# The FFT stage of a gated S4 and dense-layer backward pass: four groups' powers in one written order, with room of its own for the second group's squares

## The chip, the cores and the metric

The kernel is written in Bass and Tile for one Trainium2 chip and runs on one of its cores. The metric is the time of one execution on the device in microseconds (us), as the median of several runs; less is better. The engines are called PE (TensorE, matrix products), DVE (VectorE), ACT (ScalarE), POOL (GpSimd) and SP (SyncE, which here only issues DMAs). ACT and POOL issue DMAs too. Each engine works through its own list of instructions in order, and waits on semaphores where an instruction needs something that another engine or a DMA must have done.

## The reference

The reference is a forward and a backward pass. A gate `g` mixes two branches of an input `x` of 2048 positions by 448 channels: a state-space convolution, computed by FFT, and a dense layer with a squared ReLU. Cut to what matters here:

```python
def _A_ref(u, A_re, A_im, B_re, B_im, C_re, C_im, log_dt, Dskip):
    dt = jnp.exp(log_dt)[:, None]
    logdA = dt * (A_re + 1j * A_im)
    dB = dt * (B_re + 1j * B_im)
    P = jnp.exp(logdA[:, :, None] * l[None, None, :])
    K = jnp.einsum("dn,dnl,dn->dl", C_re + 1j * C_im, P, dB).real
    ...
    Yf = rfft2(u, zero-padded to 2 * L) * rfft2(K, zero-padded to 2 * L)
    return irfft2(Yf)[:, :, 0, :L] + u * Dskip
def _B_ref(x, w1, b1, w2, b2):
    r = relu(x @ w1 + b1)
    return (r * r) @ w2 + b2
def _fwd_reference(x, ...):
    g = sigmoid((x * gate_w).sum(-1, keepdims=True))
    return g * _A_ref(x, ...) + (1 - g) * _B_ref(x, ...)
out, vjp = jax.vjp(_fwd_reference, all arguments but B_x)
return (out, *vjp(grad_out))
```

`P` holds, for each of 448 channels and 256 states, the powers of one complex number for 2048 positions. The kernel never writes `P` out: it squares the complex numbers eleven times (levels k = 0 to 11, the powers 1, 2, 4, ... 2048) and builds small tables from the levels.

## The kernel before, in words

**Where the change lies.** The program has a start (loads, the first FFT step of `U` and of the gated gradient `DA`, the transposed copies), the FFT stage that the change touches, a long periodic stage (the tables of 14 chunks of channels between the steps of the dense layer), and an end (weight gradients, inverse FFTs, outputs). Up to the line `tc.manual_schedule()` a scheduler orders the instructions; from there on each engine's order is the order in which the code is written. The last instructions of the start, the transposed copies, are merged with the first of the FFT stage.

**Powers.** `powers(gr)` (L572) is a generator for one group of four chunks of channels (the fourth group has two). It yields once after a first copy (L583) and once after each of the levels k = 0 to 11, 13 steps in all. A level copies the present power into the group's record (L588, ACT), squares real and imaginary part into a scratch buffer `sqr` (L597, ACT), multiplies them into the next imaginary part (L598, DVE) and subtracts the squares for the next real part (L599, DVE). Level k = 4 adds four products on DVE (L591 to L594). Behind the last level POOL stores the record to HBM (`rec_d`, L602). Groups one and three keep their record in the tile `F` (`F17`) and their squares in `P` (`P14`, `W0` in the code). Groups two and four keep record and powers in `R` (`R32`, `RA`), and their squares in `S` (`S25`, `SB`). Each of these tiles had another use just before: the staged output of the first FFT step of `DA` lies in `R[0:10752]` until it is stored to HBM (`gd<-R`), and two blocks of the transposed gradient lie in `S[8192:12288]` until they are spilled to HBM (`DBT_d<-S`, L478). Right behind the stage `F` and `R` become the room of the tables.

**Spectra, products, inverse.** `load_spectrum(q, w)` loads a quarter q of what the first FFT step stored for `U` (w = 0, into tile `X`) or `DA` (w = 1, into `Y`). `spectrum(q, w, between)` makes the quarter's spectrum on PE in four pieces (`fwd2_steps`, L269), each emptied from PSUM by casts on ACT and DVE (L218, L219, L228, L230) into the tile `K`, and calls `between` after each; then POOL stores it (`sp<-K`, L624). The products of the two spectra (L293, DVE) go to the tile `D`, the first inverse step (L308, PE) takes them from there, and SP stores its result (`hd<-st` or `hd<-S`, L312).

**The order.** `levels` is the row of all groups' steps, and `PW(n)` takes the next n of it. Before, `pair_of` runs groups one and two in turn, step by step, and then three and four; a generator's end counts as a step of its own. There are 6 steps ahead of the first spectrum, 4 in it, 8 ahead of the second, 4 in it, 4 behind it, 4 in each of the six spectra that follow, and the rest (`PW(100)`) behind the loop. So groups one and two are done (26 levels' steps) when the first products begin, and the last levels of three and four come behind the last inverse step.

**Behind the stage.** SP loads the first chunk's record (`rec<-rec_d`, L741) and the stage's results (`D<-hd`, `P<-hd`, L317); DVE seeds the tables with copies (L728, L729, L764); ACT spreads the record's levels into `F` (L749 to L760); DVE builds the tables (L696, L697, L710 to L719); meanwhile POOL fills `X`, `Y`, `R` and `K` with constants (L677 to L683), once these tiles are free.

Of the kernel before, what the change touches and what calls it, by code (L numbers as in the profile page):

```python
# [32 lines left out]
NLEV = 12  # L33
RS = 1792
# [299 lines left out]
def kernel(ctx, tc, A_u, A_A_re, A_A_im, A_B_re, A_B_im, A_C_re, A_C_im, A_log_dt, A_Dskip,  # L334
# [124 lines left out]
    SB = K.t("S25", [P, 12800])  # L459
# [21 lines left out]
    RA = K.t("R32", [P, 16384])  # L481
# [9 lines left out]
    W0 = K.t("P14", [P, 7168])  # L491
# [76 lines left out]
    def powers(gr):  # L568
        nch = min(4, NCH - 4 * gr)
        cs_ = slice(4 * gr, 4 * gr + nch)  # L570
        n = nch * W2
        rb, cb, qb = psets[gr % 2]  # L572
        R = rb.rearrange("p (c r) -> p c r", c=4)[:, 0:nch]
        sd, lx, ly = fields(R)
        cur = [cb[:, 1024 * i:1024 * i + 1024].bitcast(fp32) for i in range(2)]
        sqr = qb.bitcast(fp32)

        def halves(ap):
            return ap[:, 0:2 * n].rearrange("p (t c w) -> p t c w", t=2, w=W2)

        def paired(ap):
            return ap[:, 0:2 * n].rearrange("p (c t w) -> p c t w", t=2, w=W2)
        S.copy(sd[:, :, 1], Wt[:, cs_])  # L583
        yield
        x, y = Lam[:, :, cs_], halves(cur[0])
        for k in range(NLEV):
            dst = sd[:, :, 3] if k == 3 else sd[:, :, 4] if k == 11 else sd[:, :, 0] if k == 4 else lx[..., LEVX[k]] if k in LEVX else ly[..., LEVY[k]]
            S.copy(dst.rearrange("p c t w -> p t c w"), x)  # L588
            if k == 4:
                ua, va = paired(cur[k % 2]), paired(sqr)  # L590
                V.tensor_tensor(out=ua, in0=Wt[:, cs_], in1=x[:, 0].unsqueeze(2).to_broadcast([P, nch, 2, W2]), op=ALU.mult)  # L591
                V.tensor_tensor(out=va, in0=Wt[:, cs_], in1=x[:, 1].unsqueeze(2).to_broadcast([P, nch, 2, W2]), op=ALU.mult)
                V.tensor_tensor(out=sd[:, :, 2, 0], in0=ua[:, :, 0], in1=va[:, :, 1], op=ALU.subtract)
                V.tensor_tensor(out=sd[:, :, 2, 1], in0=ua[:, :, 1], in1=va[:, :, 0], op=ALU.add)  # L594
            if k < NLEV - 1:
                sq = halves(sqr)
                S.activation(sq, x, ACT.Square)  # L597
                V.scalar_tensor_tensor(out=y[:, 1], in0=x[:, 0], scalar=2.0, in1=x[:, 1], op0=ALU.mult, op1=ALU.mult)  # L598
                V.tensor_tensor(out=y[:, 0], in0=sq[:, 0], in1=sq[:, 1], op=ALU.subtract)  # L599
                x, y = y, halves(cur[1 - k % 2])  # L600
            yield
        G_.dma_start(bass.AP(tensor=rec_d, offset=4 * gr * P * RS, ap=[[RS, P], [P * RS, nch], [1, RS]]), R)  # L602
# [12 lines left out]
    def load_spectrum(q, w):  # L615
        s1s[q, w] = s1r[(2 * q + w) % 4]
        K.load_s1(gd[w], q, s1s[q, w], G_ if w == 0 and q < 2 else None)

    def spectrum(q, w, between):
        sp = spw[:, 2 * (q % 2) + w]  # L620
        for _ in K.fwd2_steps(s1s[q, w], q, sp):
            between()
        dst = bass.AP(tensor=sp_d[w], offset=q * 4 * 2 * D, ap=[[16 * 2 * D, P], [1, 8 * D]])
        G_.dma_start(dst, sp.rearrange("p a r d -> p (a r d)"))  # L624

    def pair_of(g0, g1):
        live = [powers(g0), powers(g1)]
        while live:
            for g in list(live):
                if next(g, None) is None and g.gi_frame is None:  # L630
                    live.remove(g)
                    yield
                else:
                    yield
    levels = (x for g in ((0, 1), (2, 3)) for x in pair_of(*g))

    def PW(n=1):
        for _ in range(n):
            next(levels, None)
# [439 lines left out]
    for e in range(6):  # L1079
# [4 lines left out]
        for l in range(2 if e < 2 else 1):  # L1084
            q = G_ if (e + l) % 2 == 0 else nc.scalar
# [385 lines left out]
    def between(n):  # L1471
        Fl(1)
        Pg(1)
# [209 lines left out]
```

## Time and profile before

| What | Value |
|---|---|
| median of 3 runs | 812.24 us (810.79 to 814.69) |
| the profiled execution's own time | 809.82 us |
| its span in the profile | 808.0 us |
| mean granted TensorE clock | 0.879 |
| busy PE, DVE, ACT, POOL | 605.8, 614.0, 538.1, 169.5 us |
| FFT stage, first square of the second group to the last store | 88.14 to 180.32 us |

All times in the profile count from the start of the span. In a row of the instructions in order of time stand the start, the duration, the engine, the line of the code, the operation, what it writes and reads by the program's tile names, shapes, and in brackets how long the engine stood idle just before and what released it. `x2` means that two such instructions are merged into one row. A row with an engine name and a `q` is the queue of that engine, where a DMA is issued.

### The profile page before, as it was taken

The numbers are of one execution on the slowest core, as the hardware profiler recorded it, in microseconds if no ns is written. First come the engines' busy times: TensorE is split into PE (matmuls) and PEld (weight loads), VectorE is DVE, ScalarE is ACT, GpSimd is POOL, SyncE is SP. The second block draws the span as 40 slices with busy tenths as digits, with TensorE's granted clock in tenths as the row PEclk, the third lists the DMA queues.
The fourth block names the chain that finished last, engine by engine and source line by source line (L and its number), as shares of the span: only waits on it lengthen the run. The fifth ranks groups of instructions, "written<-read, shape, count | busy, mean of one in ns | idle before, by whom it ended". The sixth has DMA issues, their size and how long they took to land. (4 is left out here: it accounts for less than half of the span.)

```text
span 808.0 us, 17098 instructions
## 1 busy us (share of the span) xinstructions
PE 605.8 (75%) x6845; PEld 301.0 (37%) x6845; DVE 614.0 (76%) x947; ACT 538.1 (67%) x879; POOL 169.5 (21%) x276
## 2 busy tenths in 40 slices
PE   3677225562377889888988879889779688898987
PEld 1223002220143334443654435444545344444443
DVE  3793576996943989899799989998639692888355
ACT  0695585662378596868899779886467478455464
POOL 1222010005402130323231201011115321123212
PEclk9985556775678899999989999999989899999999
DMA  9978529449759197859875997898569999999982
GB/s 192 242 205 285 207 109 370 152 176 320 210 95 215 61 220 141 176 125 227 165 188 100 306 193 146 193 269 195 170 203 330 399 266 325 300 291 346 252 266 67
DMA packets 166318, 175.73 MB, mean 217 GB/s; under 512 B 104069, under 2 KB 144991, under 8 KB 165647
## 3 DMA queue, kind: packets, MB, share of 16 engines
q1 hardware_dynamic: 144376, 101.56, 50.4%
q0 software_dynamic: 19664, 70.21, 26.9%
q10 hardware_dynamic: 2198, 2.87, 1.6%
q8 instruction: 53, 0.87, 0.5%
q14 instruction: 27, 0.21, 0.1%
HBM read 83.67 MB, written 67.53 MB: 187 GB/s over the span
## 5 line engine op out<-in xcount | busy, mean ns | idle before, releaser
L857 ACT CAST P<-psF 128x1024 bf16<-128x1024 f32 x56 | 57.2, 1021 | 26.9 <-PE psF L855 26.7
L696 DVE TENSOR_TENSOR F<-X,F 128x1024 bf16<-128x1024 bf16 (+2 forms) x42 | 64.5, 1536 | 13.2 <-ACT X L729 8.0
L923 PEld LDWEIGHTS <-U 128*128 128x128 bf16 x448 | 40.6, 100 | 49.2 <-issue 14.6
L928 POOL DMA_DIRECT2D br_d<-D x32 | 17.5, 548 | 178.4 <-ACT D L927 173.4
L923 PE MATMUL psN<-D,U 128*128 128x448 bf16 x224 | 52.8, 378 | 2.6 <-DVE U L955 1.4
L1240 PEld LDWEIGHTS <-S 128*128 128x128 bf16 x416 | 38.9, 98 | 38.3 <-issue 9.1
L1240 PE MATMUL psX<-D,S 128*128 128x449 bf16 x224 | 47.2, 353 | 1.7 <-ACT S L1246 1.5
L923 PE MATMUL psN<-S,U 128*128 128x448 bf16 x224 | 46.8, 353 | 1.7 <-issue 1.5
L1003 PE MATMUL psN<-S,K 128*128 128x512 bf16 x168 | 42.4, 386 | 6.4 <-ACT R L830 5.9
L867 DVE TENSOR_TENSOR M<-P,psF 128x2048 bf16<-128x2048 bf16 x28 | 34.0, 1215 | 14.2 <-PE psF L813 12.8
L855 PE MATMUL psF<-R,S 41*32 41x256 bf16 x896 | 24.6, 291 | 26.3 <-DVE P L868 16.2
L1231 ACT ACTIVATE S<-psN 128x1024 bf16<-128x1024 bf16 x32 | 33.0, 1030 | 15.1 <-PE psN L1227 15.1
L1240 PE MATMUL psX<-K,S 128*128 128x448 bf16 x192 | 41.7, 362 | 1.5 <-ACT S L1243 1.5
L945 PE MATMUL psN<-S,K 128*128 128x512 bf16 x168 | 42.7, 392 | 0.2 <-ACT U L952 0.2
L269 PEld LDWEIGHTS <-M 128*64 128x64 bf16 x192 | 13.5, 127 | 73.8 <-issue 66.1
L697 DVE TENSOR_TENSOR X<-F 128x512 bf16<-128x512 bf16 (+2 forms) x42 | 35.6, 847 | 1.4
L1008 ACT ACTIVATE U<-psN 128x512 bf16<-128x512 f32 x56 | 31.0, 612 | 7.8 <-PE psN L1006 5.3
L836 ACT COPY S<-K 128x128 bf16<-128x128 bf16 x56 | 35.0, 1009 | 0.0
L868 DVE TENSOR_TENSOR P<-P,psF 128x2048 bf16<-128x2048 bf16 x28 | 34.2, 1221 | 1.0
L813 PE MATMUL psF<-ident,X 128*128 128x128 bf16 x448 | 32.6, 231 | 2.9 <-ACT P L857 2.7
L927 ACT CAST D<-psN 128x448 bf16<-128x448 f32 x32 | 17.4, 545 | 22.9 <-PE psN L923 22.8
L813 PEld LDWEIGHTS <-X 128*128 128x128 bf16 x448 | 28.7, 104 | 9.6 <-issue 8.4
(353 smaller groups left out, 1611.1 us busy)
## 6 DMA issues: line engine op xcount, KB each, us to landing
hd<-st SPq DMA_DIRECT2D x18, 448.0 KB, 3.1
sp<-K POOLq DMA_DIRECT2D x8, 896.0 KB, 4.0
dhT_d<-U SPq DMA_DIRECT2D x28, 256.0 KB, 5.4
R<-sp SPq DMA_DIRECT2D x8, 896.0 KB, 11.5
S<-dhT_d POOLq DMA_DIRECT2D x14, 512.0 KB, 7.2
R<-hd SPq DMA_DIRECT2D x16, 448.0 KB, 8.8
S<-rT_d POOLq DMA_DIRECT2D x12, 512.0 KB, 7.3
rec<-rec_d POOLq DMA_DIRECT2D x11, 448.0 KB, 4.8
```

The source lines that it names most:

```text
L696: V.tensor_tensor(out=Vt[:, 0:2 * w * n], in0=run(lo, 0, [0, 2], [NA, w], [1, n]), in1=run(PX[:, 0:1], 512 * k, [2, w], [0, n], [1, 2]), o ...
L697: V.tensor_tensor(out=run(lo, n, [NA * X2, 2], [NA, X2], [1, n]), in0=run(vb, 0, [n * X2, 2], [n, X2], [1, n]), in1=run(vb, (w + X2) * n, ...
L813: T_.transpose(ps[:, t, 128 * b:128 * b + 128], Xs[c % 2][:, o_:o_ + 128], ident[:])
L836: S.copy(D2[:, :, 0, 4 * l:4 * l + 4].rearrange("p (g i) a -> p a g i", g=NG), DK[:, l::4].rearrange("p a (e g q i) -> p a e q g i", g=NG, ...
L857: S.copy(zbs[c, g // 2][:, :, g % 2].rearrange("p t h k n -> p t k h n"), psz[:].rearrange("p t (k h n) -> p t k h n", k=2, h=2))
L867: V.tensor_tensor(out=pr.rearrange("p t g h k n -> p t (g h k n)"), in0=zv, in1=xv, op=ALU.mult)
L868: V.tensor_tensor(out=zv, in0=zv, in1=rev_dim(xv, 1), op=ALU.mult)
L923: T_.matmul(ps[:, 0:D], lhsT=hblk[:, j, P * tt:P * tt + P], rhs=ws[:, j, :], start=(w == 1 and j == 0), stop=(j == FT - 1))
L945: T_.matmul(pss[k][:], lhsT=w1w[:, dt, j * P:j * P + P], rhs=UT[:, dt, 512 * lb:512 * lb + 512], start=(dt == 0), stop=False, skip_group_c ...
L1003: T_.matmul(pss[k][:], lhsT=w2Tw[:, jp, dt, k], rhs=dblk[:, dt], start=(dt == 0), stop=False, skip_group_check=True)
L1231: S.activation(hn(i)[:, 8 * th:8 * th + 8, :], ps[:], ACT.Square if i < FT else ACT.Copy)
L1240: T_.matmul(ps[:, 0:w], lhsT=hn(i)[:, t, :], rhs=(DB2[:, t, :] if i < FT else U[:, t, 0:w]), start=(t == 0), stop=(t == LT - 1))
```

## The change

Three things change, all in the FFT stage. The squares of groups two and four move from `SB[:, 10240:11264]` to `RA[:, 10752:11776]`, behind the staged output. `pair_of` goes, and a list of turns takes its place: group one alone for seven steps (its first copy and k = 0 to 5), then groups one and two in turn for six steps each, then group two alone for its last seven (k = 5 to 11), then groups three and four in turn. The end of a generator, with its store, now belongs to its last step, so there are 52 steps and not 56. And they are handed out differently: 6 steps ahead of the first spectrum, 4 in it and 6 behind it make the sixteen ahead of the second spectrum, which has none; then two after each piece in the loop's first two rounds, one in the third, and none in the last.

```diff
-    psets = [(Fp[:, 0:4 * RS], RA[:, 14336:16384], W0[:, 3584:4608]), (RA[:, 0:4 * RS], RA[:, 8704:10752], SB[:, 10240:11264])]
+    psets = [(Fp[:, 0:4 * RS], RA[:, 14336:16384], W0[:, 3584:4608]), (RA[:, 0:4 * RS], RA[:, 8704:10752], RA[:, 10752:11776])]
...
-    def pair_of(g0, g1):
-        live = [powers(g0), powers(g1)]
-        while live:
-            for g in list(live):
-                if next(g, None) is None and g.gi_frame is None:
-                    live.remove(g)
-                    yield
-                else:
-                    yield
-    levels = (x for g in ((0, 1), (2, 3)) for x in pair_of(*g))
+    pws = [powers(g) for g in range(4)]
+    turns = [0] * 7 + [0, 1] * 6 + [1] * 7 + [2, 3] * 13
+    def run_levels():
+        seen = [0] * 4
+        for g in turns:
+            seen[g] += 1
+            next(pws[g])
+            if seen[g] == NLEV + 1:
+                assert next(pws[g], 1) == 1
+            yield
+    levels = run_levels()
...
     spectrum(0, 0, PW)
     load_spectrum(2, 0)
-    PW(8)
-    spectrum(0, 1, PW)
+    PW(6)
+    spectrum(0, 1, lambda: None)
     load_spectrum(2, 1)
-    PW(4)
     for q in range(4):
+        n = (2, 2, 1, 0)[q]
...
-            spectrum(q + 1, 0, PW)
+            spectrum(q + 1, 0, lambda: PW(n))
...
-            spectrum(q + 1, 1, PW)
+            spectrum(q + 1, 1, lambda: PW(n))
```

Three places show what moves. The first is ACT's list at the end of the transposed copies (L476). `F` and `R` are the records of the first and second group, `P` first the start values and then the first group's squares, `S` the transposed blocks and, before, the second group's squares. Before:

```order
L583 COPY F_87_654<-P_39_272 128x4x128
L476 COPY S_8_163<-psX_577 128x4x256
L583 COPY R_9_164<-P_39_272 128x4x128
L588 CAST F_87_654<-P_39_272 128x2x4x64
L597 ACTIVATE P_39_272<-P_39_272 128x512
L588 CAST R_9_164<-P_39_272 128x2x4x64
L476 COPY S_8_163<-psX_602 128x4x256
L476 COPY S_8_163<-psX_627 128x4x256
L597 ACTIVATE S_8_163<-P_39_272 128x512
```

And now, at the same place, up to the second group's first copy and first square:

```order
L583 COPY F_87_654<-P_39_272 128x4x128
L588 CAST F_87_654<-P_39_272 128x2x4x64
L476 COPY S_8_163<-psX_577 128x4x256
L597 ACTIVATE P_39_272<-P_39_272 128x512
L588 CAST F_87_654<-R_9_164 128x2x4x64
...
L476 COPY S_8_163<-psX_602 128x4x256
L588 CAST F_87_654<-R_9_164 128x2x4x64
L476 COPY S_8_163<-psX_627 128x4x256
...
L583 COPY R_9_164<-P_39_272 128x4x128
...
L597 ACTIVATE R_9_164<-P_39_272 128x512
```

The first group's levels moved in between the transposed copies, the second group's start moved behind them and behind the first spectrum's casts, and its squares go to `R`, where no spill is waited for.

The second place is ACT's list at the end of the second group. `st` is the inverse step's result, `K` the spectra; in the names `F` and `R` the third and fourth group follow the first and second. Before:

```order
L588 CAST F_87_654<-R_9_164 128x2x4x64
L588 CAST R_9_164<-R_9_164 128x2x4x64
L218 CAST K_88_655<-psN_104_829 128x448
L218 CAST K_88_655<-psN_107_845 128x448
L583 COPY F_87_654<-P_39_272 128x4x128
L218 CAST K_88_655<-psN_109_854 128x448
L583 COPY R_9_164<-P_39_272 128x2x128
```

And now:

```order
L228 CAST st_858<-psF_859 128x896
L218 CAST st_858<-psN_113_869 128x448
L218 CAST K_88_655<-psN_115_883 128x448
L588 CAST R_9_164<-R_9_164 128x2x4x64
L597 ACTIVATE R_9_164<-R_9_164 128x512
...
L583 COPY F_87_654<-P_39_272 128x4x128
L583 COPY R_9_164<-P_39_272 128x2x128
L218 CAST K_88_655<-psN_118_905 128x448
```

The second group's last levels moved behind the first round's first inverse casts, and the fourth group's first copy (L583 into `R`) now stands two instructions behind the last one that fills the same room; the store of that room to HBM lies between them.

The third place is POOL's list at the end of the stage, with the record stores (L602), the spectrum stores (L624) and the fills behind them. Before:

```order
L602 DMA rec_d<-F_87_654 128x4x1792
L602 DMA rec_d<-R_9_164 128x4x1792
L624 DMA sp<-K_88_655 128x3584 x6
L602 DMA rec_d<-F_87_654 128x4x1792
L602 DMA rec_d<-R_9_164 128x2x1792
L677 MEMSET X_177_1327 128x64 x2
```

And now:

```order
L602 DMA rec_d<-F_87_654 128x4x1792
L624 DMA sp<-K_88_655 128x3584
L602 DMA rec_d<-R_9_164 128x4x1792
L624 DMA sp<-K_88_655 128x3584 x3
L602 DMA rec_d<-F_87_654 128x4x1792
L602 DMA rec_d<-R_9_164 128x2x1792
L624 DMA sp<-K_88_655 128x3584 x2
L679 MEMSET X_177_1327 128x64 x2
```

The second group's record moved behind a spectrum store, and the last two records ahead of the last two spectrum stores; the fills now follow a spectrum store and not a record. SP's list has the same instructions in the same order as before, and from the tables on nothing moves on any engine (lines there count two more).

More of the change, by code (lines that the diff above doesn't have):

```diff
@@ L624, in spectrum @@
         G_.dma_start(dst, sp.rearrange("p a r d -> p (a r d)"))
-    def pair_of(g0, g1):
-        live = [powers(g0), powers(g1)]
-        while live:
-            for g in list(live):
-                if next(g, None) is None and g.gi_frame is None:
-                    live.remove(g)
-                    yield
-                else:
-                    yield
-    levels = (x for g in ((0, 1), (2, 3)) for x in pair_of(*g))
+    pws = [powers(g) for g in range(4)]
+    turns = [0] * 7 + [0, 1] * 6 + [1] * 7 + [2, 3] * 13
+    assert all(turns.count(g) == NLEV + 1 for g in range(4))
+    def run_levels():
[7 more added lines that the diff above has]
+    levels = run_levels()
     def PW(n=1):
```

## The prediction

> **What bounds the kernel now.** I read the page first, then the busy time by stretch, then the waits of the stretch that the change touches, and the instructions there in order of time. The page's span is what all sums below are made against; the execution's own time is 809.82 us.
>
> ```profile
> span 808.0 us, 17098 instructions
> ```
>
> The busy time by stretch follows; after the length stand PE, weight loads, VectorE (DVE), ScalarE (ACT), GpSimd (POOL), the granted clock, the DMA share and GB/s. The boundaries are the starts of the four product steps (118.6, 138.5, 157.6, 172.9), the last store of the stage (180.3) and the first table step behind it (194.4).
>
> ```profile
> 88.10:118.60 30.50, 8.67 (x32) 2.43 (x32) 23.23 (x56) 25.75 (x49) 1.06 (x2) 0.50 0.30 109
> 118.60:138.50 19.90, 10.72 (x58) 4.60 (x59) 12.61 (x23) 10.33 (x23) 2.63 (x4) 0.59 0.92 353
> 138.50:157.60 19.10, 10.19 (x66) 4.17 (x63) 18.20 (x40) 11.64 (x26) 0.89 (x2) 0.76 0.41 157
> 157.60:172.90 15.30, 10.53 (x62) 4.55 (x59) 14.57 (x31) 12.77 (x27) 1.24 (x3) 0.74 0.48 180
> 172.90:180.30 7.40, 5.06 (x32) 2.36 (x32) 6.85 (x10) 1.77 (x4) 0.00 (x0) 0.77 0.61 222
> 180.30:194.40 14.10, 0.00 (x0) 0.00 (x0) 5.98 (x8) 4.03 (x10) 6.81 (x8) 0.58 0.99 353
> 194.40:230.00 35.60, 16.18 (x194) 9.59 (x197) 33.84 (x39) 17.07 (x23) 13.69 (x11) 0.64 0.77 200
> ```
>
> PE is nowhere the bound here. Before the products ACT paces (25.75 of 30.5). In the middle stretches DVE does (18.20 of 19.1, 14.57 of 15.3). At 118.6 to 138.5 and at 180.3 to 194.4 both idle and the DMAs are full. From 194.4 on DVE is full again (33.84 of 35.6), so whatever lets the table steps start earlier passes on.
>
> Of ACT's list of waits in this stretch (total, times, longest) the second longest is this one; the third is the one that the change names, below:
>
> ```profile
> ACT F L749 <- DMA rec_d<-F: 10.1, 1, 10.1
> ```
>
> **The change part by part.** *The second group's squares get their own room.* ACT reaches the second group's first square when the last transposed copies are done, and stands until the last spill of those transposed blocks has landed. All that ACT has queued behind it stands too, the casts that PE needs first of all.
>
> ```profile
> 70.97 1.01 ACT L476 COPY S<-psX 128x1024 bf16<-128x1024 bf16 x1 [4.86 <-PE psX L472]
> 74.53 0.62 ACT L583 COPY R<-P 128x512 bf16<-128x512 bf16 x1 [2.55 <-DMA gd<-R]
> 88.14 0.63 ACT L597 ACTIVATE S<-P 128x512 f32<-128x512 f32 x1 [7.88 <-DMA DBT_d<-S]
> ```
>
> The new room is written by nothing that is still in flight, so the 7.88 go. What is late next is the level chain itself, and here the order of steps decides. A level is a copy and a square on ACT and a subtraction on DVE:
>
> ```profile
> 103.56 0.60 ACT L588 CAST F<-R 128x512 bf16<-128x512 f32 x1
> 104.06 0.62 ACT L597 ACTIVATE P<-R 128x512 f32<-128x512 f32 x1
> 104.59 0.60 ACT L588 CAST R<-R 128x512 bf16<-128x512 f32 x1
> 104.72 0.42 DVE L599 TENSOR_TENSOR R<-P 128x256 f32<-128x256 f32 x1 [0.28 <-ACT P L597]
> ```
>
> PSUM is emptied by casts, in turn on ACT and DVE. Two groups of DVE's work from 88 to 181 (busy, mean ns of one):
>
> ```profile
> L219 DVE CAST K<-psN 128x448 bf16<-128x448 f32 x23 | 14.1, 615 | 1.5 <-PE psN L269 1.5
> L230 DVE CAST K<-psF 128x896 bf16<-128x896 f32 x7 | 7.6, 1081 | 0.0
> ```
>
> With two groups in turn a level costs ACT 1.03 (103.56 to 104.59). Alone it costs the whole chain: 0.50 to the square, 0.62 for it, 0.04 to the subtraction, 0.42 for that and 0.05 back, 1.63. No row shows a group alone, so 1.63 is an estimate from these rows; 1.03 is its floor.
>
> *To the first products.* From 71.98 (70.97 + 1.01) the first group runs alone in what was waiting time. Four levels take 4 x 1.63 less the first copy, plus 0.7 where a transposed copy holds DVE: 6.7, to 78.7. Two transposed copies with PE's transposes between them take some 3.5, from 78.2, where ACT is free, to 81.7; the next three levels, the first half done, 4.4, to 86.1. Then the new group's first copy (0.45) and seven levels in turn, 7.3, to 93.9, and the second spectrum's casts on ACT, about 3.0 by the size of DVE's: products at 96.9. They were at 118.58. But only 16 of the 52 steps are done by then, where all 26 of the first two groups were, so most of these 21.7 us are borrowed.
>
> ```profile
> 118.58 2.09 DVE L293 TENSOR_TENSOR D<-K 128x1792 bf16<-128x1792 bf16 x2
> 119.00 0.77 POOL L602 DMA_DIRECT2D rec_d<-F  x1 [2.29 <-ACT F L588]
> 119.77 0.76 POOL L602 DMA_DIRECT2D rec_d<-R  x1
> 125.59 0.62 ACT L583 COPY F<-P 128x512 bf16<-128x512 bf16 x1 [5.40 <-DMA rec_d<-F]
> 130.15 0.40 ACT L583 COPY R<-P 128x256 bf16<-128x256 bf16 x1 [3.51 <-DMA rec_d<-R]
> ```
>
> *The second group ends alone.* Its eight levels k4 to k11 now lie between the first products and their inverse. The first products (2.09), a small and a large cast and the level before (some 0.7) take 4.3; k4, with the 2.11 of its extra products (rows below) in front of square and subtraction, 3.3, to 104.5; five levels alone 8.2, to 112.7; the second products (2.0 start to start), two casts and the two DVE instructions of k10 3.8, k11's copy 0.7: its record goes out at 117.2. The very next ACT instructions start groups three and four, and the fourth needs that room back. The two stores took 6.6 (119.00 to 125.59) and 10.4 us (119.77 to 130.15) to release ACT. So the wait ends between 123.8 and 127.6; I take 126, nearer the longer row, because a spectrum store and two spectrum loads are queued beside it. The first group's store is now early, so the old 5.40 go, and the old 3.51 become about 8. Behind this wait stand ACT's casts; PE and DVE soon stand for them. The Trainium skill's page "DMA: Bandwidth & Descriptors" (Anatomy of one DMA) fits such a store with 2.0 us plus its bytes at 436 GB/s, which for 1.84 MB is 6.2; the 6.6 agrees, the 10.4 doesn't, and by the page alone the sum would end 2.6 us lower.
>
> *Second step.* From 126 ACT needs 5.4 for the fourth group's copy (0.3), two casts (0.9), two levels each of a full and a half group (2 x 1.7, an estimate from 1.03 for a full one) and the inverse's cast (0.8); products at 131.4, against 138.5, with exactly as many levels done (32 of 52). Here the borrowed time has been paid back, and 7.1 us are left.
>
> ```profile
> 145.28 2.08 DVE L293 TENSOR_TENSOR D<-K 128x1792 bf16<-128x1792 bf16 x2
> 141.07 0.41 DVE L598 SCALAR_TENSOR_TENSOR R<-R 128x256 f32<-128x256 f32 x1
> 141.41 0.41 DVE L599 TENSOR_TENSOR R<-P 128x256 f32<-128x256 f32 x1
> 142.74 0.28 DVE L598 SCALAR_TENSOR_TENSOR R<-R 128x128 f32<-128x128 f32 x1
> 142.94 0.28 DVE L599 TENSOR_TENSOR R<-S 128x128 f32<-128x128 f32 x1
> 148.35 0.68 DVE L591 TENSOR_TENSOR R<-P,R 128x512 f32<-128x512 bf16 x1
> 150.46 0.42 DVE L598 SCALAR_TENSOR_TENSOR R<-R 128x256 f32<-128x256 f32 x1
> 152.52 0.41 DVE L591 TENSOR_TENSOR R<-P,R 128x256 f32<-128x256 bf16 x1
> 153.83 0.29 DVE L598 SCALAR_TENSOR_TENSOR R<-R 128x128 f32<-128x128 f32 x1
> ```
>
> *Levels packed.* Half a step with two pairs of levels took 6.7 (138.5 to 145.28). A pair costs DVE 2 x 0.34 and 2 x 0.20, start to start: 1.08. The k4 products cost 2.11 and 1.31. Now the second step has four pairs in each half, k4 in its first. First half: 6.7 + 2.16 + 3.4 = 12.3, and 1.1 for waits (before, the half with k4 took 12.3 where its parts give 10.1). Second half: 8.9, and 1.8 because ACT needs as long there as DVE. 131.4 + 13.4 + 10.7 = 155.5; without those waits 152.6, with twice them 158.4. The third step has one pair, then none: 5.7, and 4.6 on DVE where PE (10.53 in the two halves before) needs over 5.3; I take 6.5, so 167.7, from 10.3 for the step to the old 15.3. The fourth step had none before: 7.4, so 175.1 against 180.3, a gain of 5.2.
>
> *Behind the stage.* Before, the last levels and both record stores came after the last spectrum store; now they go out at about 161 (155.5 + 5.7), 14 us ahead of it.
>
> ```profile
> 180.32 0.36 SPq L312 DMA_DIRECT2D hd<-S  x1
> 185.28 3.18 DVE L728 COPY X<-rec 128x128 bf16<-128x128 bf16 x1 [3.17 <-DMA rec<-rec_d]
> 194.37 1.09 DVE L696 TENSOR_TENSOR F<-X,F 128x1024 bf16<-128x1024 bf16 x1 [4.33 <-ACT F L752]
> 197.51 3.51 POOL L678 MEMSET R<- 128x4096 f32 x1 [8.06 <-DVE F L696]
> 198.15 2.29 DVE L696 TENSOR_TENSOR F<-X,F 128x4096 bf16<-128x4096 bf16 x1
> 208.66 0.83 ACT L749 COPY F<-M 128x768 bf16<-128x768 bf16 x1 [11.48 <-DMA M<-rec_d]
> 211.38 0.44 DVE L728 COPY X<-M 128x128 bf16<-128x128 bf16 x1
> 216.02 2.29 DVE L696 TENSOR_TENSOR F<-X,F 128x4096 bf16<-128x4096 bf16 x1
> ```
>
> From the last store to the first table step 14.05 us passed: 4.96 for the record, then the copies, then 4.33 for ACT, which stood 10.1 until the third group's record had left the table's room. That wait goes. The end is 9.7 (14.05 less 4.33) if the copies stay slow, and 6.8 (4.96, and some 1.8 for ACT's two fills) if they don't; I take 8.7, nearer the first, since GpSimd's fills still meet the copies. The table starts at 183.8 instead of 194.37: 10.6 us. The second table's record, awaited at 208.66, has 2.75 MB less before it in full DMAs, so it stays covered; were it not, the gain would shrink to that of its own load.
>
> The copies show the price of GpSimd's fills: 3.18 us at 185.28 and 0.44 at 211.38. DVE's table product took 2.29 beside such a fill (197.51) and 2.29 at 216.02. The fills of X and Y now come earlier, under the fourth step's products and casts. The Trainium skill's page "SBUF — State Buffer" (Who interferes with whom) says that copies and casts can take the port pair shared with GpSimd and then one fully blocks the other, while a two-input product does not meet a GpSimd write. Copies and products agree with these rows; no run shows a cast out of PSUM beside a fill.
>
> Sum: 809.82 - 10.6 = 799.2 for the profiled execution. The median of the runs, 812.24, stands 2.4 above it; on that base 801.6. The ends of the unknown terms: the store at 123.8 or 127.6 (-2.2, +1.6), the second step (-2.9, +2.9), the third (-1.9, +3.1), the tail (-1.9, +1.0).
>
> **The rivals.** *Only the tail is won.* The borrowed levels come back dearer: the fourth group's copy waits the full 10.4, every wait in the packed halves doubles and the third step keeps its old 15.3. That is 1.6 + 2.9 + 3.1 = 7.6 late, which eats the stage's 5.2 and 2.4 more, and the tail's 5.4 is left at 3.0; typically half of it, a gain of 5 to 7. For it: DVE is at 18.20 of 19.1 already. Against: the third step loses three pairs of levels. Time 805 to 809.
>
> *The DMAs take it back.* From 161 on the stage's two records, two spectra, their products' stores and the next stage's loads follow in one queue; if that runs at 250 GB/s instead of the 353 of 180.3 to 194.4, the second table's record lands where it did, at 208.66. Gain 0 to 2, time 810 to 812. Against: the bytes are the same and start earlier.
>
> *The fills block DVE: slower.* If casts out of PSUM stand for a GpSimd fill as the copies did, the fills of X, Y and R (some 10.3 us) lie under the fourth step and the fill of K (6.2) under its last casts and the copies behind. The stage then ends 16.5 later, at 191.6, and the table starts at 191.6 + 6.8 = 198.4: 4.0 later than now, 816.3. It decides as soon as a cast at the fourth step reads over 3 us instead of its 0.6 or 1.1. Against: the products run on beside fills.
>
> *Nothing happens.* Another wait holds ACT until 88 in place of the old one, the second group's first copy waiting for the spectrum stage's last store. It would give 812. Before, that store released ACT at 74.5, and now it is asked for at 86.
>
> **How the numbers follow.** Forecast 0.64; only the tail 0.18; DMAs 0.09; fills 0.06; nothing 0.03. A measurement of this kernel can tell about 0.5%, 4 us. Of the forecast nearly all and of the second case 0.14 are faster by more: 0.77. Slower by more: half of the fills and a little for mishaps, 0.05. The rest, 0.18, is no change. The forecast's own range is 797 to 805; to hold 8 in 10 it must take in the second case's body, so 796.5 to 808.5.
>
> **What would show it.** Right: no ACT wait for the transposed spill; products first at about 97 and again at 131; one ACT wait of about 8 us for a record store near 118 to 126; the four-pair halves 13 and 11 us; the last spectrum store near 175; no 10 us ACT wait for the record behind it; DVE full from 184. The forecast is wrong if the second products come after 135, if a packed half takes over 16, or if DVE waits for the second record.

## The result, and the profile after

The changed kernel ran in 806.64 us (median of 9, 802.02 to 808.06) beside 811.56 us of the kernel before (median of 9, 810.03 to 814.69). The ratio is 0.992, with an interval of 0.990 to 0.995, so some 6 us are won (0.0078 x 811.56 = 6.3). A second set of runs of the same two kernels, e11 below, gives about 4.0 (0.0049 x 812). The forecast was 801.6, a gain of 10.6. The profiled execution took 806.01 against 809.82, and this is the span of its page:

```profile
span 804.2 us, 17075 instructions
```

The busy time by stretch, with the columns of the table in the prediction; the boundaries are the new places of the same events.

```profile
72.00:96.30 24.30, 12.89 (x80) 5.82 (x82) 18.08 (x40) 21.02 (x39) 2.66 (x5) 0.57 0.72 269
...
116.60:127.80 11.20, 1.68 (x8) 0.62 (x8) 0.97 (x3) 0.28 (x1) 0.76 (x1) 0.50 0.94 337
...
133.20:157.20 24.00, 13.69 (x64) 5.82 (x64) 22.79 (x56) 18.69 (x43) 1.06 (x2) 0.53 0.31 116
157.20:169.70 12.50, 9.01 (x60) 3.96 (x59) 11.56 (x19) 8.62 (x17) 2.79 (x6) 0.73 0.81 313
169.70:176.40 6.70, 3.69 (x32) 1.64 (x32) 6.68 (x9) 1.62 (x4) 6.64 (x7) 1.00 1.02 379
176.40:185.40 9.00, 0.00 (x0) 0.00 (x0) 2.42 (x3) 2.43 (x4) 8.15 (x4) 0.68 0.78 237
185.40:220.50 35.10, 14.92 (x163) 8.50 (x164) 34.01 (x40) 13.75 (x20) 3.64 (x7) 0.60 0.84 214
```

Read the second row first: for 11.2 us PE, DVE and ACT are all but idle (1.68, 0.97 and 0.28 busy) while the DMAs are full (0.94). The other rows are as dense as hoped: DVE 22.79 of 24.0, 11.56 of 12.5, 6.68 of 6.7. The instructions behind that, in order of time:

```profile
74.03 0.62 ACT L588 CAST F<-R 128x512 bf16<-128x512 f32 x1 [1.25 <-DVE R L599]
75.67 0.62 ACT L588 CAST F<-R 128x512 bf16<-128x512 f32 x1 [0.49 <-DVE R L599]
...
96.31 2.08 DVE L293 TENSOR_TENSOR D<-K 128x1792 bf16<-128x1792 bf16 x2
...
116.65 0.76 POOL L602 DMA_DIRECT2D rec_d<-R  x1 [6.37 <-ACT R L588]
127.83 0.40 ACT L583 COPY R<-P 128x256 bf16<-128x256 bf16 x1 [10.95 <-DMA rec_d<-R]
129.75 0.42 DVE L599 TENSOR_TENSOR R<-P 128x256 f32<-128x256 f32 x1 [12.17 <-ACT P L597]
133.18 2.08 DVE L293 TENSOR_TENSOR D<-K 128x1792 bf16<-128x1792 bf16 x2
...
146.62 2.08 DVE L293 TENSOR_TENSOR D<-K 128x1792 bf16<-128x1792 bf16 x2
...
157.16 2.08 DVE L293 TENSOR_TENSOR D<-K 128x1792 bf16<-128x1792 bf16 x2
...
169.70 4.08 DVE L293 TENSOR_TENSOR D<-K 128x1792 bf16<-128x1792 bf16 x4
169.76 3.85 POOL L680 MEMSET Y<- 128x4096 f32 x1
173.71 0.61 DVE L219 CAST st<-psN 128x448 bf16<-128x448 f32 x1
174.19 3.82 POOL L680 MEMSET R<- 128x4096 f32 x1
174.24 1.08 DVE L230 CAST st<-psF 128x896 bf16<-128x896 f32 x1
176.44 1.77 SPq L312 DMA_DIRECT2D hd<-S  x1
178.52 6.21 POOL L685 MEMSET K<- 32x3584 f32 x2
182.98 2.05 DVE L730 COPY X<-rec 128x128 bf16<-128x128 bf16 x1 [6.60 <-DMA rec<-rec_d]
185.41 1.14 DVE L698 TENSOR_TENSOR F<-X,F 128x1024 bf16<-128x1024 bf16 x1
```

The wait for the transposed spill is gone, a level alone costs 1.64 (74.03 to 75.67), the first products come at 96.31. Then the one new wait: the second group's record leaves at 116.65, and the fourth group's first copy stands for it until 127.83, with DVE 12.17 behind. The first table step comes at 185.41 instead of 194.37, 8.96 earlier.

What becomes of those 8.96 shows at a place 40 us on. Towards the end of the first table ACT fills the fields of the second one. It needs the second record, and room that DVE's last product of the first table (L713 before, L715 after) still reads. Before:

```profile
207.70 2.50 DVE L713 TENSOR_TENSOR F<-Y,F 128x1024 bf16<-128x1024 bf16 x4
210.29 1.47 ACT L757 COPY F<-M 128x1536 bf16<-128x1536 bf16 x1
...
233.11 0.43 DVE L840 TENSOR_TENSOR S<-S,vw 128x512 bf16<-128x512 bf16 x1 [3.78 <-ACT S L836]
```

After:

```profile
198.78 2.50 DVE L715 TENSOR_TENSOR F<-Y,F 128x1024 bf16<-128x1024 bf16 x4
201.76 0.83 ACT L751 COPY F<-M 128x768 bf16<-128x768 bf16 x1 [14.28 <-DMA M<-rec_d]
203.33 1.46 ACT L759 COPY F<-M 128x1536 bf16<-128x1536 bf16 x1
...
226.14 0.42 DVE L842 TENSOR_TENSOR S<-S,vw 128x512 bf16<-128x512 bf16 x1 [5.61 <-ACT S L838]
```

Before, DVE was done with the room at 210.20 and ACT's fill began at 210.29. The record (208.66, in the prediction) and the two fills ahead of this one, some 1.6 us, ended at the same instant, so it was just in time. After, DVE is done at 201.28, 8.9 earlier, but the record lands only 6.90 earlier, at 201.76, and the fill begins at 203.33, 6.96 earlier. The **first scaled product** (L840, now L842) keeps that and comes 6.97 earlier. It is the yardstick below, since it stands behind the whole stage and repeats within a microsecond: two executions of the change have it at 226.14 and 225.84, two of the room alone at 223.56 and 222.62. There is one trace of the kernel before, and all differences to it rest on that one.

### The profile page after: what moved, and what is told of

Its sections match the earlier page's. It is cut to its first block, busy times and chain, and to the rows that moved or that the text cites. A ratio compares the mean times of both kernels' runs of the same rounds, so it can differ in the third digit from the quotient of the medians.

```text
span 804.2 us, 17075 instructions
## 1 busy us (share of the span) xinstructions
PE 605.3 (75%) x6818; PEld 301.3 (37%) x6845; DVE 612.7 (76%) x947; ACT 538.1 (67%) x879; POOL 169.2 (21%) x276
## 5 line engine op out<-in xcount | busy, mean ns | idle before, releaser
L925 PE MATMUL psN<-D,U 128*128 128x448 bf16 x224 | 55.5, 393 | 3.2 <-DMA D<-in_B_w_dram 2.8
L1005 PE MATMUL psN<-S,K 128*128 128x512 bf16 x154 | 40.4, 380 | 6.6 <-ACT R L832 5.6
L947 PE MATMUL psN<-S,K 128*128 128x512 bf16 x155 | 40.6, 388 | 1.1 <-issue 0.6
L308 PEld LDWEIGHTS <-cb_MI 64*128 64x128 bf16 x256 | 14.5, 104 | 54.5 <-issue 46.3
L815 PE MATMUL psF<-ident,X 128*128 128x128 bf16 x448 | 32.5, 231 | 2.7 <-ACT P L859 2.5
```

What stands on the lines that cost most here:

```text
L815: T_.transpose(ps[:, t, 128 * b:128 * b + 128], Xs[c % 2][:, o_:o_ + 128], ident[:])
L925: T_.matmul(ps[:, 0:D], lhsT=hblk[:, j, P * tt:P * tt + P], rhs=ws[:, j, :], start=(w == 1 and j == 0), stop=(j == FT - 1))
L947: T_.matmul(pss[k][:], lhsT=w1w[:, dt, j * P:j * P + P], rhs=UT[:, dt, 512 * lb:512 * lb + 512], start=(dt == 0), stop=False, skip_group_c ...
L1005: T_.matmul(pss[k][:], lhsT=w2Tw[:, jp, dt, k], rhs=dblk[:, dt], start=(dt == 0), stop=False, skip_group_check=True)
```

## The experiments

The ratios are to the kernel before, each with its 95% interval. The experiments are numbered e1 to e12. Those of one group (e1 to e4, e5 to e8, e9 to e12) ran on one chip with one set of runs of the kernel before. A theory is named by the letter that it has in the quoted expectation.

### The room alone, twice, beside the change

In e1, and again in e12, one line of the kernel before is changed:

```
-... (RA[:, 0:4 * RS], RA[:, 8704:10752], SB[:, 10240:11264])]
+... (RA[:, 0:4 * RS], RA[:, 8704:10752], RA[:, 10752:11776])]
```

> The kernel before, with only the second group's squares in their own room; the order of the steps stays the old one. Theory A (the room takes away a wait of 7.88 us, and the new order adds an earlier end of the levels on top): no wait for the transposed spill, the first products about 7 us earlier than 118.58, near 111.5, the two record stores awaited on ScalarE for about 5.4 and 3.5 us as before, the wait of some 10 us for the third group's record behind the stage stays, last store of the stage near 173.5, first table step near 187.4, ratio to the kernel before 0.992 to 0.995. Theory B (the order is what wins, the room only lets the next wait come): ratio 0.998 to 1.000, and another wait near 74 to 88 stands in its place.

Measured: 0.985 (0.980 to 0.990), better than either theory. Its instructions in order of time:

```profile
109.24 2.09 DVE L293 TENSOR_TENSOR D<-K 128x1792 bf16<-128x1792 bf16 x2
...
120.81 0.40 ACT L583 COPY R<-P 128x256 bf16<-128x256 bf16 x1 [3.52 <-DMA rec_d<-R]
129.20 2.08 DVE L293 TENSOR_TENSOR D<-K 128x1792 bf16<-128x1792 bf16 x2
...
170.35 0.36 SPq L312 DMA_DIRECT2D hd<-S  x1
184.78 1.09 DVE L696 TENSOR_TENSOR F<-X,F 128x1024 bf16<-128x1024 bf16 x1 [4.83 <-ACT F L752]
198.88 0.83 ACT L749 COPY F<-M 128x768 bf16<-128x768 bf16 x1 [11.29 <-DMA M<-rec_d]
200.70 1.47 ACT L757 COPY F<-M 128x1536 bf16<-128x1536 bf16 x1 [0.15 <-DVE F L713]
223.56 0.43 DVE L840 TENSOR_TENSOR S<-S,vw 128x512 bf16<-128x512 bf16 x1 [3.81 <-ACT S L836]
```

With the old order, the room gives 9.34 at the first products (118.58 to 109.24) and 9.55 at the first scaled product, more than the whole change. So the view that the order adds to the room fell. The two were then run side by side, the change as e11 and the room alone as e12.

> The changed kernel once more, on the same chip and in the same rounds as e12, to set it beside the room alone. Theory A (given the room, the new order costs more than it wins, by the wait for the second group's record): the ratio here is 0.003 or more above e12's. Theory B (e1's better number was its chip): within 0.003 of e12's.

> The kernel before with only the own room for the second group's squares, as e1, beside the changed kernel. Theory A: ratio to the kernel before 0.984 to 0.989, at least 0.003 below e11's; first products near 109.2, first scaled product near 223.6. Theory B: within 0.003 of e11's.

Measured: the change 0.995 (0.992 to 0.998), median 807.79 of 12; the room alone 0.991 (0.987 to 0.994), median 803.15 of 10; the means differ by 4.2 us, with a standard error of 1.1. Both ratios are higher than in the first runs (0.992 and 0.985), and the room's misses its expected 0.984 to 0.989, but their distance, 0.004, is theory A's: given the room, the new order costs. In the first traces the second products stand at 133.18 with the change and at 129.20 with the room alone, and the first scaled products at 226.14 and 223.56. The table does start about as early (185.41 and 184.78), though the last store of the stage is 6.1 later (176.44 and 170.35). The shorter way from that store to the table is real, 8.97 instead of 14.43, so 5.5 us. But the second record's way from that store shortens by only 3.2 (28.53 to 25.32). In e1 ACT's fill begins at 200.70, when DVE is done with the room; with the change it begins at 203.33, when the record and the two fills ahead of it are done.

### The order alone

In e2 the changed kernel has the old room again (the `-` line above in place of the `+` line).

> The changed kernel, with the second group's squares in their old room again. Theory A (the room is needed): the wait for the transposed spill is back, at least 2 us long, and what follows is as much later; ratio to the kernel before 0.995 to 1.000. Theory B (the order alone does it, since the second group's first square is now asked for only near 88 us, when the spill has landed): wait under 1 us, first products at 96.3 to 97.3, ratio as the changed kernel's, 0.990 to 0.9945.

```profile
90.14 0.63 ACT L597 ACTIVATE S<-P 128x512 f32<-128x512 f32 x1 [1.93 <-DMA DBT_d<-S]
228.16 0.43 DVE L842 TENSOR_TENSOR S<-S,vw 128x512 bf16<-128x512 bf16 x1 [5.59 <-ACT S L838]
```

Measured: 0.988 (0.982 to 0.994). The wait for the spill is down from 7.88 to 1.93, since the square is asked for later; the first products come at 98.17, the first scaled product 4.95 earlier than before. The wait is nearly theory A's, the ratio is theory B's or better, so the truth lies between them: the order alone does about half of what the room does at the yardstick, and the two don't add up (4.95 and 9.55 alone, 6.97 together).

### The third group alone, so that nobody waits for the record

In e3 only the list of turns of the changed kernel differs:

```
-turns = [0] * 7 + [0, 1] * 6 + [1] * 7 + [2, 3] * 13
+turns = [0] * 7 + [0, 1] * 6 + [1] * 7 + [2] * 7 + [2, 3] * 6 + [3] * 7
```

> The changed kernel, with the third group alone for seven steps before the fourth begins (and the fourth alone for its last seven), so that the fourth's first copy, which needs the room of the second group's record, comes only in the second step. Theory A (the 11 us on ScalarE for that record's store are the price of the change): no ScalarE wait over 4 us between 110 and 135, second products at 124 to 128 instead of 133.2, last store of the stage at 170 to 173 instead of 176.4, first table step near 180, ratio to the kernel before 0.984 to 0.989. Theory B (the wait only fills time that VectorE's and ScalarE's work of the later steps would take anyway, or a wait for another transfer takes its place): last store at 175 or later, ratio 0.990 to 0.995.

```profile
126.13 2.09 DVE L293 TENSOR_TENSOR D<-K 128x1792 bf16<-128x1792 bf16 x2
167.78 0.36 SPq L312 DMA_DIRECT2D hd<-S  x1
216.10 0.42 DVE L842 TENSOR_TENSOR S<-S,vw 128x512 bf16<-128x512 bf16 x1 [4.63 <-ACT S L838]
```

Measured: 0.979 (0.974 to 0.985). The wait is gone from ACT's list, the second products come 7.05 earlier than with the change, and the first scaled product 10.04 earlier. This is theory A, and more than it asked for (0.984 to 0.989). Experiment e8 has the same third group alone with the own room and the old order of the first two (`turns = [0, 1] * 13 + [2] * 7 + [2, 3] * 6 + [3] * 7`), its steps handed out as before:

> The kernel before with the own room for the second group's squares, the first two groups in turn from the first step as before, and only the third group alone for seven steps ahead of the fourth. Theory A (the own room and the order of the first two groups do the same job twice, and what the new order adds is only that the levels end earlier and so their record stores): the first products near 109.2 as in e1, no ScalarE wait for the second group's record, a wait of 0 to 5.4 us for the first group's, last store of the stage at 168 to 170.5, ScalarE's wait of some 10 us for the third group's record gone or under 5 because that record goes out earlier, ratio to the kernel before 0.979 to 0.985. Theory B (the first group alone is worth something of its own): last store at 170.5 or later, ratio 0.985 or more, while e3 has 0.979.

```profile
221.50 0.43 DVE L842 TENSOR_TENSOR S<-S,vw 128x512 bf16<-128x512 bf16 x1 [5.60 <-ACT S L838]
```

Measured: 0.987 (0.983 to 0.992), last store 171.21. So the new order of the first two groups, with the way its steps are handed out, is worth 5.4 (221.50 to 216.10) once nobody stands for the second record's store, and costs 2.58 (223.56 to 226.14) while ACT does. The ratio and the last store are theory B's. Theory A is not wholly out, though: 3.4 of the 5.4 stand at the last store (171.21 and 167.78), and the rest comes behind it, where the fourth group's record leaves at 172.68 in e8 and at 154.83 in e3, and the second table's record is asked for at 181.82 and 176.26. That part may well be what theory A names, the levels that end earlier.

### Why that store took 11 us

In e10 the two loads of the fourth step's spectra are issued one step later:

```
-        if q == 0:
+        if q == 1:
             load_spectrum(3, 0)
```

and likewise for `load_spectrum(3, 1)`.

> The changed kernel, with the two loads of the fourth step's spectra issued in the second step instead of the first, so that they do not run beside the second group's record store. Theory A (the store takes 11.2 us because those 1.6 MB are moved beside it; alone it would take the 6.6 of the first store in the kernel before): ScalarE's wait for it ends at 122.5 to 124.5 instead of 127.8, second products at 128 to 130 instead of 133.2, first scaled product 2.5 to 4.5 us earlier than 226.1, ratio to the kernel before 0.9865 to 0.990. Theory B (the store is slow by its own shape or by its queue): the wait ends at 127 or later and the ratio is the changed kernel's, 0.990 to 0.9945.

```profile
122.44 0.40 ACT L583 COPY R<-P 128x256 bf16<-128x256 bf16 x1 [6.20 <-DMA rec_d<-R]
127.79 2.08 DVE L293 TENSOR_TENSOR D<-K 128x1792 bf16<-128x1792 bf16 x2
221.16 0.43 DVE L842 TENSOR_TENSOR S<-S,vw 128x512 bf16<-128x512 bf16 x1 [5.86 <-ACT S L838]
```

Measured: 0.985 (0.977 to 0.993). The store left at 116.01 and released ACT at 122.44, 6.43 us instead of 11.18 (116.65 to 127.83), and the 5.4 won at the second products arrive as 4.98 at the first scaled product. This is theory A, a little beyond its ranges: the two loads were the price. They are 896 KB each, 1.8 MB and not 1.6. The Trainium skill's page "DMA: Bandwidth & Descriptors" (Anatomy of one DMA) gives 2.0 us plus the bytes at 436 GB/s, an estimate of 6.2 for this store. The 6.43 of the store without the loads agrees; the 11.18 of the store beside them lies 5.0 above it.

### Who paces behind the stage

In e4 the second record's load stands right behind the first one's, ahead of the eight loads of the halves:

```
     load_rec(0)
+    rec0 = rec
+    load_rec(1)
+    rec1, rec = rec, rec0
     for q in range(4):
         K.load_hs(hd[0], q, hss[q])
...
-    load_rec(1)
+    rec = rec1
     tables(0)
```

> The changed kernel, with the second table's record loaded right behind the first one's, ahead of the eight loads of the inverse's halves. Theory A (behind the stage ScalarE paces, and the wait for the second record that ended at 201.8 is what lost 2 us of the 8.8 won): ScalarE's first field copy of the second table at 195 to 198, its casts of the inverse's small sums start near 204 instead of 206.2, first scaled product of VectorE near 224 instead of 226.1, ratio to the kernel before 0.988 to 0.9905. Theory B (VectorE paces there, as the prediction said): the ratio stays the changed kernel's, 0.990 to 0.9945. Theory C (the DMAs pace): the eight loads land as much later as the record's own load, some 2 us, and nothing is won or up to 1 us lost.

```profile
201.19 1.47 ACT L759 COPY F<-M 128x1536 bf16<-128x1536 bf16 x1 [8.13 <-DVE F L715]
223.94 0.43 DVE L842 TENSOR_TENSOR S<-S,vw 128x512 bf16<-128x512 bf16 x1 [3.67 <-ACT S L838]
```

Measured: 0.986 (0.981 to 0.991). The record no longer holds ACT, the first two fills are done by 193.07, and the third waits 8.13 for DVE's last product of the first table. So 2.2 us come back (226.14 to 223.94), about the 2.0 by which the record had fallen behind DVE, and then DVE's first table paces. That is theory A's way for the record and theory B's pace behind it.

In e7 one more DVE product of 128x4096 (its result is overwritten) stands within the second table:

```
     tables(1)
+    V.tensor_tensor(out=Vt[:, 0:4096], in0=Ys[0][:, 0:4096], in1=Ys[0][:, 4096:8192], op=ALU.mult)
```

> The changed kernel with one VectorE product of 128x4096 more (its result goes into a scratch room that is overwritten; it is extra work) between the two tables' steps of the second chunk, 2.29 us by its like. Theory A (VectorE is not the bound between 185 and 226): the first scaled product stays at 226.1 within 0.5, VectorE's wait ahead of it falls from 5.6 to 3.3, the ratio to the kernel before stays 0.987 to 0.993. Theory B (VectorE paces there): the first scaled product at 228.4, the ratio 0.003 higher.

```profile
226.78 0.42 DVE L842 TENSOR_TENSOR S<-S,vw 128x512 bf16<-128x512 bf16 x1 [3.54 <-ACT S L838]
```

Measured: 0.990 (0.987 to 0.994). DVE's wait falls from 5.61 to 3.54. The first scaled product moves by 0.64, a little over theory A's 0.5, of which 0.35 stood at the first table step already (185.76). Some 2 of 2.29 us are swallowed: in the second table DVE isn't the bound. Its busy share of 34.01 in 35.1 hid that, because the stretch ends at 220.50, just where DVE's wait for ACT begins (226.14 less 5.61 is 220.53).

### The fills and the copies

In e6 GpSimd's two fills of K are written behind the first table step:

```
-    for h in range(2):
-        G_.memset(KW[64 * h + 32:64 * h + 64, NA * D:].bitcast(fp32), 0.0)
...
-    tables(0)
+    step_x(0, 2, 0)
+    for h in range(2):
+        G_.memset(KW[64 * h + 32:64 * h + 64, NA * D:].bitcast(fp32), 0.0)
+    for i in (1, 2):
+        step_x(0, 2 << i, i)
```

> The changed kernel, with GpSimd's two fills of K (6.2 us) issued behind the first table step instead of ahead of it, so that they do not meet VectorE's copies of the record. Theory A (ScalarE paces behind the stage, through the second record and the inverse's small sums; VectorE has over 5 us to spare there): the copies take 0.4 to 0.7 us instead of 2.05, the first table step comes 0.5 to 1.2 us earlier than 185.4, and the first scaled product stays at 226.1 within 0.5; ratio to the kernel before as the changed kernel's in the same call's terms, 0.987 to 0.993. Theory B (VectorE paces there, as the prediction said): the first scaled product comes as much earlier as the first table step.

Measured: 0.991 (0.988 to 0.995), and it told nothing: GpSimd waits for no step of DVE's here, so the fill, written behind the first table step, still began at 179.03 and the copies took 2.03. So the fill has to be tied to something of DVE's. First e3 and e4 were put together, as e5:

> The changed kernel with the third group alone for seven steps (as in e3) and the second table's record loaded ahead of the inverse's halves (as in e4). Theory A (the ScalarE wait for the second group's record and the wait for the second table's record are two separate losses): last store of the stage near 167.8 as in e3, ScalarE's field copies of the second table no longer wait for their record, first scaled product of VectorE at 213 to 214.5 instead of e3's 216.1, ratio to the kernel before 0.975 to 0.979. Theory B (with the stage this early the DMAs pace, so the second load ahead only delays the halves): first scaled product at 216 or later, ratio 0.979 to 0.983.

Measured for e5: 0.978 (0.973 to 0.983), first scaled product at 215.40. Theory A's place, 213 to 214.5, was missed: ACT's third fill waits 8.12 for DVE there, whose first table step came at 176.81 only, though the record had released the copies at 172.98. The third of these copies took 3.71 beside the fill of K (0.73 in e9, without a fill).

In e9, on top of e5, GpSimd's fill of R is now issued behind the copies and tied there by a small DVE fill in the same room (`fill_y` holds the two fills of L680 and L681):

```
     seeds_y(0)
+    V.memset(Ys[1][:, 0:2], 0.0)
+    fill_y(Ys[1])
```

> As e5 (third group alone, second record first), and GpSimd's fill of R is issued behind VectorE's copies of the first record (a two-element VectorE fill in the same room makes it wait), the fill of K ahead of it, so that no fill is running when the copies start. Theory A (the copies stand until the running fill ends, and behind it VectorE's first table paces ScalarE's fields of the second): the three copies take 0.4 to 0.8 us each, first table step at 174.5 to 175.5 instead of e5's 176.8, first scaled product 1 to 2 us before e5's 215.4, ratio to the kernel before 0.974 to 0.979. Theory B (the copies were slow because the DMAs were full, or ScalarE's fields set the first table step anyway): first table step at 176.3 or later, ratio as e5's, 0.976 to 0.981.

```profile
165.96 6.19 POOL L687 MEMSET K<- 32x3584 f32 x2
173.02 0.45 DVE L732 COPY X<-rec 128x128 bf16<-128x128 bf16 x1 [4.68 <-DMA rec<-rec_d]
174.71 1.08 DVE L700 TENSOR_TENSOR F<-X,F 128x1024 bf16<-128x1024 bf16 x1 [0.48 <-ACT F L756]
213.52 0.42 DVE L844 TENSOR_TENSOR S<-S,vw 128x512 bf16<-128x512 bf16 x1 [3.77 <-ACT S L840]
```

Measured: 0.978 (0.973 to 0.982), median 791.8 beside 813.26. The table starts 2.10 earlier than in e5, and the first scaled product comes 1.88 earlier. The traces show theory A's times; the ratio alone fits both theories. This is the fastest version found, 2.2% ahead of the kernel before, but its interval overlaps with those of e5 and e3.

## Why the prediction was right in kind and too large

| event | before | forecast | after | the term, forecast and measured |
|---|---|---|---|---|
| level alone | – | 1.63 | 1.64 | as said |
| first products | 118.58 | 96.9 | 96.31 | as said |
| ACT's wait for the record ends | 130.15 | 126 | 127.83 | +1.83 |
| second products | 138.50 | 131.4 | 133.18 | 5.4 and 5.35 behind the wait |
| packed halves | – | 13.4, 10.7 | 13.44, 10.54 | 24.1 and 23.98 |
| fourth step | 172.9 | 167.7 | 169.70 | 12.2 and 12.54 |
| last store | 180.32 | 175.1 | 176.44 | 7.4 and 6.74 |
| first table step | 194.37 | 183.8 | 185.41 | 8.7 and 8.97 |
| first scaled product | 233.11 | 10.6 earlier | 226.14 | 6.97 earlier |

*Right.* The spill's wait goes; the levels alone, the packed halves, the third and fourth steps and the way to the table each cost what was worked out, within 0.7. The casts out of PSUM ran at 0.61 and 1.08 beside the fills (rows at 173.71 and 174.24, the second wholly inside the fill of R), so the rival in which fills block casts is out, as is the one in which nothing happens. The forecast's own range, 797 to 805, missed the 806.64. The wide one holds it because it had been stretched for the rival in which only the tail is won, so that hit is in part luck.

*The store's wait was mis-sized.* The prediction took 126 between 123.8 and 127.6; it was 127.83, just past the longer end, though the store left 0.55 earlier than forecast. It took 11.18, longer than both rows that the prediction had, 6.6 and 10.4. The two loads beside it (issued at 115.06 and 115.92) were named as the reason to go nearer the longer row, and e10 shows that they are the reason; their price was set too low. The wait ends 1.83 late, and the table starts 1.6 late.

*The last step failed.* It was: the second table's record "stays covered", DVE is full, and whatever is won passes on. The record lost 2.0 us against DVE and took over, and e7 shows that DVE isn't the bound in the second table; e4 gives 2.2 back, and its later products stay 1.5 to 2.2 ahead of the change's up to 580 us. The profile of before held the warning: ACT's fill of the second table began at 210.29, right behind DVE's 210.20, and the record with its two fills ended at the same instant. A cover with 0.1 us to spare is no cover when one side moves by 9 and the other by 7. The prediction did name the way out in half a sentence, "were it not, the gain would shrink to that of its own load", and this is what happened: the record landed 6.90 earlier, and the yardstick comes 6.97 earlier. It gave this case no number in the sum or the range. In the rival of the DMAs the record lands where it did and nothing is won, which is not what happened. Of its three signs of being wrong, two stayed away (second products at 133.18, halves of 13.44 and 10.54); the third, a wait for the second record, came, with ACT standing for it (14.28, at 201.76) and DVE behind ACT.

*The rival "only the tail is won"* gave 805 to 809, and the median lies in it, but not by its way: the wait was the full one, as it said, but no half came dearer and the third step was short. At the last store 3.9 of the forecast 5.2 were left and not a loss of 2.4. Of the tail, 5.1 arrived at the table (14.05 to 8.97), but only 3.0 at the second record, which is the one that counts (28.34 to 25.32 behind the last store).

*What was not seen at all* is the comparison of the parts. The prediction put the first group's order and the room into one sum. Apart, the room gives 9.55 at the first scaled product, and the order on top of it takes 2.58 back, through the wait that it pulls onto ACT while two spectrum loads are under way: with these loads elsewhere (e10) the change has the first scaled product at 221.16, 2.40 ahead of the room alone.

*What stays open.* Behind the first scaled product the gain of the profiled execution did not stay where it was: it went from 6.97 to 8.7 (at 251 us, by the products of L867) and 5.8 (at 281), stood at 6.2 at 400 and at 3.8 at the end (spans 808.0 and 804.2). In e1's execution it went from 9.55 to 11.1, 11.0, 11.4 and 8.3 (span 799.7). So the 6 us of the runs agree with the 6.97 partly by chance. The drop at 281 is the one in the last section; why the gain rose ahead of it and why the late part gave some back was not tried.

## What to carry to other kernels

Cost the parts of a change apart: here one line of storage did more than the whole, and the reordering paid on top of it only once ACT no longer stood for a store (e3) or that store ran without two loads beside it (e10). Before a gain is passed on through a full engine, find the wait that ends last at the next meeting point, and write down its slack, the time by which the other side could be later; where both sides end at the same instant, the slack is zero. And when a room is to be reused, look at what else is in the DMAs while the store that frees it is under way.

## What the runs showed of the hardware

**A copy from SBUF to SBUF on DVE ends with GpSimd's fill.** Before, the fill and the copy (the copy's row, 185.28 and 3.18 long, stands in the prediction):

```profile
184.31 3.84 POOL L678 MEMSET Y<- 128x4096 f32 x1
```

The fill ends at 188.15, the copy at 188.46. After, the fill of K ends at 184.73 and the copy at 185.03. In e1 they end at 178.06 (174.22 and 3.84) and 178.37 (175.49 and 2.88). Each time the copy ends 0.30 or 0.31 us behind the fill, and with no fill running it takes 0.45 (e9). Casts out of PSUM (1.08 at 174.24, as the 1081 ns on average before) and two-input products (2.29 at 198.15 and at 216.02) run on beside fills unchanged. The Trainium skill's page "SBUF — State Buffer" (Who interferes with whom) says that a copy or cast can hold a port pair shared with GpSimd and that one then fully blocks the other. The copies agree; the casts that read PSUM don't show it.

**The same work met a low granted clock in some executions and not in others.** This is one stretch of the same work, up to DVE's wait for sixteen transposes on PE, first with the change and then before:

```profile
269.90:275.50 5.60, 5.60 (x42) 3.11 (x42) 2.94 (x4) 3.68 (x5) 0.47 (x1) 0.52 0.32 69
```

```profile
278.10:281.40 3.30, 3.30 (x42) 2.04 (x42) 3.27 (x5) 3.30 (x5) 0.50 (x1) 0.99 0.11 35
```

At a granted clock of 0.52 PE takes 5.60 us for it, at 0.99 it takes 3.30. The sixteen transposes (L815, before L813) took 1.82 and 1.07, and DVE lost 2.8 us of its lead: its product before this stretch comes 8.61 earlier than in the kernel before, the one behind it 5.84 earlier. Between these two products lie 9.7 to 9.8 us in ten of the fourteen traces and 12.2 to 12.5 in four: both of the change, e2 and e4. The change with a small addition and all of it up to 1 us later (e6 and e7) has 9.70 and 9.82. What decides it was not tried. Two executions of the change stood 0.3 us apart at the yardstick and end 3.1 apart (spans 804.2 and 807.3), so the end of one execution is no measure of a gain of this size.
